# Attention through a packed set, then a squared-ReLU layer: second softmax's scores in 32x32 tiles, seven groups of block products, stores as steps of the plan on three queues

## The chip, the cores and the metric

The kernel runs on one core of a Trainium2 chip. The metric is the device time of one execution in microseconds. Before the change the median of five runs is 249.96 us (248.67 to 250.8).

A core has five engines that run side by side, each with its own instruction queue: TensorE (PE, matrix products; loading its weights is listed as PEld), VectorE (DVE), ScalarE (ACT), GpSimd (POOL) and SyncE (SP). Transfers between the device's memory and the core's are issued from the queues of SP, ACT and POOL.

## The reference

Eight batches of eight heads, 576 tokens, 64 numbers per head. A short set `p` of 32 rows per head attends to the 576 keys and values, and gives 32 packed rows; then the 576 queries attend to these packed rows. The result, 4608 tokens of 512 numbers, goes through a layer of 2048 hidden units.

```python
def _attn_ref(q, k, v, p):
    scale = 1.0 / np.sqrt(q.shape[-1])
    def sm_attn(qq, kk, vv):
        s = scale * np.matmul(qq, kk.transpose(0, 1, 3, 2))
        s = s - np.max(s, axis=-1, keepdims=True)
        a = np.exp(s)
        a = a / (np.sum(a, axis=-1, keepdims=True) + 1e-09)
        return np.matmul(a, vv)
    p_packed = sm_attn(p, k, v)
    return sm_attn(q, p_packed, p_packed)

def _moe_ref(x, w_in, w_out):
    r = np.maximum(x @ w_in, 0.0)
    return (r * r) @ w_out
```

All inputs and outputs are float32; the kernel computes its products in bf16.

## The kernel before, in words

**Stages of a batch.** The heads of a batch are two "quads" (`qd`) of four heads `h`. Loads (`Loads`) bring k, q and v in as bf16 through POOL's queue, batch 0's k as float32 through ACT's and SP's. DVE transposes k (`tr_k`, L273) and q (`tr_q`, L267). `S1` is the first softmax's scores (`s1`, `s1_rest`), with `p` spread into a block-diagonal tile `pT_bd`; ACT takes their exponential. `PV` multiplies with v and sums the rows. `XT` copies the product out as `pp` (`extract`), takes the reciprocal of the sums (`recip`), and `pq_block` copies the packed rows, as 32x32 blocks, into a block-diagonal tile `pq_bd` of 128x128 weights.

`M` (`m`, L354) multiplies the packed rows by w_in, in tiles of 64x32: eight matmuls of 512 columns, each into its own 32 partitions, for each 512 columns of w_in; from batch 1 on two such sets in a row. The layer's first product then needs no attention output: `f1_mm` (L417, halves in batch 0: L426) multiplies the softmax weights by `M`.

`S2` (`s2`, L379) is the second softmax's scores: for each quad, four matmuls of 288 columns with `pq_bd` as 128x128 weights (two halves of the queries, two halves `dh` of the head's 64 numbers). ACT takes the exponential (`s2_exp`); `N` sums over the 32 packed rows with a block of ones (L391), takes the inverse on ACT as logarithm and exponential (L396, L399), and DVE multiplies (`n_mul`, L405). In batch 0 (`SPLIT`) S2 and N are done in two halves of the queries.

`R` is `f1_mm` with its ReLU, on ACT or DVE; `F1` is the square (`f1_sq`, L452, DVE), into `gT`, which holds two batches. `F2` is the second product of the layer. A tile `t` of 128 tokens (36 in all) is 16 matmuls of 512 columns (`f2_mm`, L501), a copy out, and four stores, one to each of four 32-row parts (`store`, L477). From tile 15 on, four tiles at a time are a group (`GROUPS`): seven products of halves instead of eight (`prod`, L560, 16 matmuls of 256 columns each), with sums of the squares (`g_sum`, L546, names `WS`) and of w_out (`w_sum`, names `WT`) made on DVE, and the products copied or added into the output tile (`prod_out`). Tile 35 is done in two column halves (`f2_last`, L487).

**What sets the order.** Each piece of work is a `Step` with stages, dependencies, and slots that it takes and gives; some pieces may go to DVE or ACT. The order of all pieces, and the engine of each, was found beforehand and stands in the file as a compressed list (`ORDER`); `Plan.run` issues the pieces in that order. Each engine works its own list in order. Steps of type "-" and "DMA" issue nothing. So an instruction that waits holds up everything that was issued later on the same engine, stores and loads too.

**Buffers that matter here.** Two `h` buffers in PSUM (scores, sums and `f1` products of all wide batches, `M`), two `a` buffers (S1, PV, tiles 2 and 3), two output buffers `o0`, `o1`; eight load buffers for k and q (`kqb`); one tile `qT` for the transposed queries, so that `Tq` of a batch waits for S2 of the batch before; three output tiles `o_sb`.

**Stores.** They are issued in the step that copies or adds the last part of a tile, four in a row; all on SP, but for half of those of tile 35 that go to ACT's queue:

```python
(eng or nc.sync if i % 2 else nc.sync).dma_start(dst, src[32 * i:32 * i + 32])
```

Of the kernel before, what the change touches and what calls it, by code (L numbers as in the profile page):

```python
# [14 lines left out]
P = 128  # L15
# [11 lines left out]
GROUPS = (15, 19, 23, 27, 31)  # L27
SPLIT = (0,)

# [20 lines left out]
class Plan:  # L50
# [21 lines left out]
    'c-jrtgMu9i6a~Pm)5-X86x+6K+qP}nwr$(CZQHhY>nn=LD1aOaqU01vp_H0J$V=%+DJCT*AH}2W<fbUfL>Vb7m7*+^n<`Km%0R^^0VSb=RFq0n'  # L72
    'Z7NUIsSCBDj<k@PP#c;-J!v3qp%FBJ4p2>ML_?`QHK*|un-Wr9s!Fw}FO{T<)Qmb%H(E<$X)>LpO|*-i(rQ{y_h=f;p-VKMmeDmjLZ|30U8L)z'
    'e4NhGce+iF$i)xo1;yg$^qvy&JNiN?`78aQtn6VQ7v}_=ge&nsiou20&vCdMXW;BymuqnYp2&H*2)E&;+@4o(DXzdhcmNOQZJdnLaCI)vRk<&Z'
    '<;i@Et8r}}%p-Ul@8w3^lIQSO{>KqAgBS35e!_3~7x(1;ypeqpTT)A2DJ12@CE=1lp7Td0DJJEmp%j$jQd@5E1Afi-`6++m(o#j5$$S3JK~hm_'
    'N_)wm*|mVqmnE`JmdkqCD>=2G*4DMMSq{r$StVQLtNanuESg)(YcVaWEwr3g*S`8spniQI&*ZKA6jqm((n{J%^J#Idr%a$=5{f~Q6o=xw;!;vd'
    'Mk!pmD2!a>p<a}O^3XT>O&z!kAL6UrPiDz=xh=!J<21EpF+YX7V!0wH+BJZ7l5sm0xg>2h5v8I6RD{Y=6{<sHD3lX&J}%4McnR;|ef)z>Qc5<d'
    'ERE!{ypteJuA_9C&eq+U&dOLNTW={TEv2Vyl$ml;KFUvpsIaRHm7wCTQ8bmN&`g?5i|H>3$K(Ka1c$hzxD40eDqN2nb2IMB6L>05<3&81=eh6j'
    'W4^~<_$UA2K=DYVM0v7ELQgz7BuC|l9GBB_R<6iZxhZ!%ujRQslv-L>8)-9btZlTNcGND~%{xMSX>adKeXXzboxayk`dPp0PyOX(3o`PxvbNUF'
    '23kk!W<zYajk57J)28?q`dU&uS9=;p6KOQ<pna}AbeV3@eR8vx<8omx%@z3(zu=edzwAh`#FylfUXIC0&jqQY4ZIDtwYK+m&^|iAJ5WFB7yasO'  # L80
    'W4)|{4YFZ2#-`aUo8x<9@9e#=ELEmTRE=s-U1~^8sU9_^*3_9APz!2Hov15yr+ze;dQfi~LL(_LC*@R}meX+-F2Kb&8|UJpT$$JKdfvcWcsuXr'
    'yX=)~e1ln%NDj#@`K72-kgC#Fx=I)6E(2t!e3EbSTSx;mSUnm`!!$zUX(1h><8`b~)~PyEm*`5JrE_(g9#gMHSbR%jnJt^;vG$hF3Ro$tVH<6;'
    '?Xcap#}3*l`)Nn)m_4u%^r1o2pN7*on&g^J^Jp$DaxJBmw1zg&M%qe8=>#34b98~OxbDysdPcA54Sl4~^pk#(<F3OE-SxSJyDfL(&fJ}QaUbr-'
    'LwFdE<}o~pr|?Xk#mjgxujV~`fDiH!KF+83G@s)Oe3=VNS*a!Uq=7V%rqV*%NGItjeWb4p@(hvTGDgP9B$?`&BGYA_ERqGXLe|Je*(BR!r|gzJ'
    'vR`h=eYq!3<f*)rSMpx|N=)@?Y>lf4yzw=OH<_l?)S6b)X(r94xipU!)}mTk%V=etuM2gNF7+<gRk~W&=?2}bTXeg3r|!|cx?d0K5k0CW^pu{}'
    'b9zxP=~ca^H}$sO*9ZDYpXv+!r|J`PEWm;-(84U-Vq08GV96|vrLv5c--=pED{G~#f>pMvR?TW!ZL4SXt&uIYRleo6+D_VeyI_~?s@<@gcE|49'
    'Q~P1R?U(&C0pK7ef)I)@xZy_x!V%?9h$KjiWd4*$gS5ziOvs9C$ca42k3uMl;wXjED2Ixuf*Poe`e=nlXo~jegpTOr?~Y!WMayYB9j3eViilJ2'
    'Kpx5Cc`a|^GklS6b8G1(qh*53mDRFC4$5cwB|c5BS+%5A)S9|hH|Zfgt(Wz>KGx^zw|JJ&3R)d&Xw9s(U9^Yx+7yBCA|BEqI|`!&YN91NqX&jz'
    '0j;9Vw3|-T8G1=S2pq_f9FLQ8PR`E-xu$ysZKJ)kpAOM2`aqv3h=Vyc$LHLfhf8otZp}+*9UY|ebd_$>1A0u%VI0oUoSM^fCeF+`+)cPSx8jc6'
    'n+New9>vpnF3;zMyp&h+X5Pgo+!^^HXOIF?L`q3rSt$4PjegKS>b7W0ZaJ*8^|Qe?)F#?=TV~sApB=UncFk_tJxhel$c-|njJjxuCYXX*Sb}xf'  # L90
    'gzeakBe;!+Sk9|>9dG5Gyq^#AQ9j9M`4V5@>wJ@+@hcAXyybWNfj{#%{>>_o7!p$gBt*i*Eq;lXxDrd^NFqrrNhO)2kW`XJ(n>nXD48U)WR>ia'
    '%ac>`NIoecC8dm1l4??2YDgWaFO8+Sw3JrT!P8DUN@wXNJ*2nvmw_@^hRFySDWhbpjF*WrS*FPhnJKenjx3dBvQjq47TGSlWS<<66LLzf$r(8('
    '=jEc@kh}6o9?J`PBOm0We39?+Lqr{~Y77n35DitghHIooX|%@CgqlbbYf??2dA+GLjb_x$nnUwz5iOw=w2D^MYFb0<YZGm%ExpaPm3G#y+Fg5S'
    'Pwl7ub&w9$Av#ot=|~-|6TK63l1|a-Iz#8^JYArRb(yZvHM(9m>Q>#M=e@ghpB~V|dR$NH8NHx)yjS#w-qO4JP@m{CeXB9;oBq(>`d7_hF)YM<'
    '7HTf@SfoW+EQ@1_EQKYuq?XdsT6)W1nJla2wd|JDa#?OGWQDDW6|)jn+{#&bt7uiMy4A9}*4!FcV{2kft%bF;PS(YG__|tm>uJ5MkM*_wHo!*M'
    'NE>ZqZJbT8NjBN0+G5`fn{9J#p3S!fw#b&)3R`JwY^|-c4YtX)*jC$V+ijQawf%O$4%tyVZfESYowajz$*$OSyKQ&vx$luZwkP(?Uf4@}WpC}9'
    '?}L4`Pxjfq*jM{*e~j?g7={=KKrmeJAQpUxL^NU}4&ov{5+Id7DUu@vQX@SwA`5aLA95it3ZNj0pcqP`EGnQpDxoT>p*m`z4(g!+8lxGSqXk-{'
    '4cej|I{3SwE4ra4dZRD;p+5#<00v<&hF~a$V+2NGw0{)FU@XRAJSJcwCSfWjV;ZJo24-S5=3p-7V;&Y@Ar@gVmSP!}V<lE#6;@*n)?z(2U?a9*'
    'Gqz$Ic3>xVVGs6VzkeSN;2;j+FplCFj^iXw;1o{d49?;l&f@|u`7h!!uHY)J;W}>MChp)C?&2Qq;{hJwF`nQVp5i%P;3Zz+HQwMY-s2rU;3Gca'
    'Grr&}zTqdn;|G4>H~!!+{(+qT^Wmst4jjjc;ly-;oB$`#33fu9P$$fBIc~?}cpabPcfy?rC(?;>qMiQ$NqrJ;'  # L100
# [3 lines left out]
def kernel_impl(tc, q, k, v, p, w_in, w_out, out):  # L104
# [15 lines left out]
    with ExitStack() as ctx:  # L120
# [25 lines left out]
        pq_bd = [consts.tile([P, 896], BF16, name=f"pq_bd{i}") for i in range(2)]  # L146
# [11 lines left out]

        def bd(t, h, dh):
            return both(t, dh * BDW + 32 * h, P + (-32 if h % 2 else 32), 32)[32 * h:32 * h + 32]  # L160
# [7 lines left out]
        def setup():  # L168
# [4 lines left out]
            nc.vector.memset(kT[:, :, GM * P + 64:], 0.0)  # L173
            nc.vector.memset(v_t[0][64:, :, GM * D:], 0.0)
            nc.vector.memset(v_t[1][64:, :, GM * D:], 0.0)
            nc.vector.memset(pq_bd[0][:, :BDW + 2 * P], 0.0)

        def setup_rest():
            nc.gpsimd.memset(ones_bd, 0.0)
# [414 lines left out]
        def stage(*pieces):  # L594
            return list(pieces)
# [336 lines left out]
```

The softmax here doesn't subtract the row's maximum and nothing guards it: scores larger than these inputs give would overflow.

## Time and profile before

| what | us |
|---|---|
| median of five runs | 249.96 |
| the profiled execution | 249.17 |
| its span, first to last instruction | 247.2 |
| PE busy | 225.5 |
| DVE busy | 186.1 |
| ACT busy | 157.7 |
| POOL busy | 60.2 |
| mean granted TensorE clock | 0.995 |

The span is what the trace covers; some 2 us of the execution lie around it. Busy times overlap between engines. A matmul's record starts when it begins and ends when its results are written, so records of neighbouring matmuls overlap: the distance from one start to the next tells what a matmul costs, and a busy PE is not a PE at its peak. In the kernel's rows the output names stand left of the arrow and the inputs right of it.

### The profile page before, as it was taken

The page shows a single profiled execution, that of the slowest core. Times are in us where ns is not written, and L with a number is a line of the kernel's source. Part 1 is how long each engine was busy: PE and PEld are TensorE (multiplying, and loading weights), DVE is VectorE, ACT ScalarE, POOL GpSimd, SP SyncE. Part 2 cuts the span into 40 slices and gives each one's busy share as a digit, 9 for nine tenths or more (in the row PEclk, how much of TensorE's full clock was granted, in tenths as well). Part 3 has the DMA queues.
Part 4 walks back from the last instruction along what each step waited for, and adds up shares of the span by engine and source line. Part 5 has one row for each costly group of instructions (what it writes and reads, how often), then busy time and mean ns, then how long its engine had stood idle before and what let it go on. Part 6 is the DMA issues. An engine that isn't in the chain of part 4 may idle for free.

```text
span 247.2 us, 5373 instructions
## 1 busy us (share of the span) xinstructions
PE 225.5 (91%) x2096; PEld 160.1 (65%) x2096; DVE 186.1 (75%) x325; ACT 157.7 (64%) x273; POOL 60.2 (24%) x120
## 2 busy tenths in 40 slices
PE   0679998996999999999999999999999999999970
PEld 0525564573654666666556888887787888888860
DVE  4875649876998696779787989898897798767410
ACT  3368577885887766785788887877775756400010
POOL 7697576562093003452100000000000000000000
PEclk9999999999999999999999999999999999999998
DMA  7999999999999945699611010033014001504243
GB/s 221 199 183 205 205 202 208 204 245 220 193 121 203 244 92 95 95 181 213 118 45 42 13 32 3 0 88 88 3 32 124 18 3 44 128 1 110 63 110 102
DMA packets 27160, 29.01 MB, mean 117 GB/s; under 512 B 5760, under 2 KB 18816, under 8 KB 27136
## 3 DMA queue, kind: packets, MB, share of 16 engines
q0 software_dynamic: 19472, 17.99, 46.0%
q1 hardware_dynamic: 7328, 9.97, 14.9%
q10 hardware_dynamic: 336, 0.72, 0.9%
q8 instruction: 16, 0.26, 0.4%
q14 instruction: 8, 0.07, 0.1%
HBM read 37.22 MB, written 9.44 MB: 189 GB/s over the span
## 4 chain that ended last, share of the span: by engine, by line
PE 78%; DMA 11%; DVE 3%; ACT 3%; issue 1%; POOL 1%; SPq 0%; DVEq 0%
PE ps_o L560 24%; PE ps_h L417 20%; PE ps_o L501 16%; DMA q_b<-in_q_dram 4%; DMA k_b<-in_k_dram 4%; PE ps_m L354 4%; PE ps_h L426 3%; PE ps_a L283 3%; PE ps_s L379 3%; PE ps_pp L316 2%; DMA p_f<-in_p_dram 2%; PE ps_s L391 1%; DMA out_dram<-o_sb 1%; PE ps_a L501 1%; DVE kT L273 1%
## 5 line engine op out<-in xcount | busy, mean ns | idle before, releaser
L445 ACT ACTIVATE r<-ps_h 128x576 bf16<-128x576 f32 x99 | 63.7, 650 | 26.6 <-PE ps_h L417 24.6
L417 PE MATMUL ps_h<-a,M 128*128 128x288 bf16 x448 | 71.1, 286 | 0.0
L501 PE MATMUL ps_o<-w_out_b,gT 128*128 128x512 bf16 x208 | 58.7, 379 | 0.7 <-DMA w_out_b<-in_moe_w_out_dram 0.7
L417 PEld LDWEIGHTS <-M 128*128 128x128 bf16 x448 | 43.6, 98 | 16.3
L452 DVE TENSOR_TENSOR gT<-r 128x1152 bf16<-128x1152 bf16 x64 | 46.8, 747 | 6.1 <-ACT r L445 3.8
L560 PEld LDWEIGHTS <-wS 128*128 128x128 bf16 x320 | 31.0, 98 | 4.7 <-issue 0.4
L501 PEld LDWEIGHTS <-gT 128*128 128x128 bf16 x240 | 22.3, 98 | 17.0 <-issue 3.4
L560 PE MATMUL ps_o<-wT,wS 128*128 128x256 bf16 x240 | 30.5, 273 | 0.0
L238 POOL DMA_DIRECT2D v_r<-in_v_dram x32 | 19.0, 597 | 33.9 <-DVE wT L525 16.0
L164 ACT CAST M<-ps_m 128x1024 bf16<-128x1024 f32 (+1 forms) x26 | 23.1, 915 | 6.2 <-PE ps_m L354 4.9
L267 DVE STREAM_TRANSPOSE qT<-q_b 128x1152 bf16<-128x1152 bf16 (+1 forms) x18 | 21.9, 1229 | 6.1 <-DMA q_b<-in_q_dram 4.2
L560 PEld LDWEIGHTS <-gT 128*128 128x128 bf16 x240 | 23.3, 98 | 3.8 <-issue 0.4
L164 ACT COPY o_sb<-ps_o 128x512 f32<-128x512 f32 (+1 forms) x15 | 8.6, 572 | 22.7 <-PE ps_o L560 19.6
L560 PE MATMUL ps_o<-w_out_b,gT 128*128 128x256 bf16 x160 | 20.9, 273 | 0.0
L166 DVE COPY o_sb<-ps_o 128x512 f32<-128x512 f32 (+1 forms) x20 | 13.4, 671 | 8.1 <-PE ps_o L560 3.6
L283 PE MATMUL ps_a<-pT_bd,kT 128*128 128x128 bf16 x128 | 10.3, 233 | 8.3 <-DVE kT L273 8.3
L386 ACT ACTIVATE e<-ps_s,rD 128x576 bf16<-128x576 f32 (+1 forms) x18 | 12.2, 687 | 8.3 <-PE ps_s L379 8.2
L166 DVE CAST M<-ps_m 128x1024 bf16<-128x1024 f32 (+1 forms) x10 | 11.2, 1118 | 7.2 <-PE ps_m L354 6.5
L283 PEld LDWEIGHTS <-kT 128*128 128x128 bf16 x128 | 8.7, 105 | 10.7 <-DVE kT L273 8.7
L573 DVE TENSOR_TENSOR o_sb<-ps_o,o_sb 128x512 f32<-128x512 f32 x15 | 10.3, 689 | 6.2 <-PE ps_o L560 5.0
L379 PE MATMUL ps_s<-qT,pq_bd 128*128 128x288 bf16 x64 | 11.4, 304 | 3.4 <-DVE qT L267 2.1
L405 DVE SCALAR_TENSOR_TENSOR a<-e,rD,ls 128x576 bf16<-128x576 bf16 (+1 forms) x18 | 13.4, 742 | 1.4 <-ACT ls L399 1.2
(72 smaller groups left out, 302.8 us busy)
## 6 DMA issues: line engine op xcount, KB each, us to landing
out_dram<-o_sb SPq DMA_DIRECT2D x140, 64.0 KB, 1.7
k_b<-in_k_dram POOLq DMA_DIRECT2D x14, 288.0 KB, 8.9
q_b<-in_q_dram POOLq DMA_DIRECT2D x14, 288.0 KB, 9.0
v_r<-in_v_dram POOLq DMA_DIRECT2D x16, 160.0 KB, 8.6
v_r<-in_v_dram POOLq DMA_DIRECT2D x16, 128.0 KB, 7.1
w_in_b<-in_moe_w_in_dram POOLq DMA_DIRECT2D x8, 256.0 KB, 8.5
w_out_b<-in_moe_w_out_dram POOLq DMA_DIRECT2D x8, 256.0 KB, 8.6
k_f<-in_k_dram ACTq DMA_DIRECT2D x1, 576.0 KB, 4.2
```

The lines of the kernel that those rows point to most:

```text
L164: nc.scalar.copy(dst, src)
L166: eng.tensor_copy(dst, src)
L238: nc.gpsimd.dma_start(self.vr[32 * i:32 * i + 32, h0:h1, :n * D], src[:, :, J0[i] * D:(J0[i] + n) * D])
L267: nc.vector.transpose(self.qT[:, qd, :, j0 * 32:j1 * 32].rearrange("p dh (j a) -> p j dh a", a=32), self.t.qb[qd][:, j0 * D:j1 * D].rearra ...
L283: nc.tensor.matmul(ps[:, g * P:(g + 1) * P], lhsT=self.kT[:, qd, g * P:(g + 1) * P].bitcast(BF16).rearrange("p (t two) -> p two t", two=2) ...
L379: nc.tensor.matmul(ps[:, c], lhsT=self.pq[:, blk(qd, dh)], rhs=self.qT[:, qd, dh, n0:n0 + HALF], start=(dh == 0), stop=(dh == 1))
L405: nc.vector.scalar_tensor_tensor(out=self.a2[:, qd, n0:n1].rearrange("p (c n) -> p c n", n=HALF), in0=self.e2[qd, hf], scalar=self.rD[:, q ...
L417: nc.tensor.matmul(ps[:, c, :HALF], lhsT=a.M[:, qd, fb * FB:(fb + 1) * FB], rhs=a.a2[:, qd, c * HALF:(c + 1) * HALF], start=(qd == 0), sto ...
L445: nc.scalar.activation(dst, src, ACT.Relu)
L452: eng.tensor_tensor(out=gT[:, fb - 1:fb + 1, o:o + S], in0=r, in1=r, op=ALU.mult)
L501: nc.tensor.matmul(po[t], lhsT=gT[:, fb, n0:n0 + P], rhs=w_out_b[:, fb, :], start=(fb == 0), stop=(fb == NFB - 1))
L560: nc.tensor.matmul(ps[:, u * EH:(u + 1) * EH], lhsT=lhs, rhs=rhs, start=(n in (1, 2, 4) and kk == 0 and u == 0), stop=(kk == KB - 1 and u ...
```

## The change

- **S2 in tiles.** `pq_bd` is gone. `packed` takes each head's 32x32 weights where they are: for two of the eight pairs (head, `dh`) from `pp` itself, for the other six from a small tile `pq`, which `pq_part` fills with six block copies a batch instead of eight. `s2` computes both quads together: for each half of the queries and each `dh`, eight matmuls of 32 rows, 32 columns of weights and 288 columns, head `h` of quad `qd` from row part `h` into partitions `32 * (h ^ qd)`. A wide batch takes both `h` buffers at once; 32 matmuls instead of eight.
- **Buffers.** `qT` has two buffers, and `Tq` waits for S2 two batches back; `e1` and `e1r` have one instead of two; `e2` has two for each quad instead of three in all. Two memsets of `pq_bd` go.
- **Groups.** Tiles 7 to 14 become two more groups; `GROUPS` has seven.
- **Squares** may go to ACT (`Square`); the list puts ten of 64 there.
- **Stores** are steps of their own (`store_step`), of two stores each, on SP, from tile 8 on also POOL, from tile 31 on also ACT: 92 on SP, 50 on POOL, 6 on ACT, where it was 144 on SP and 4 on ACT.
- **The order.** `ORDER` is a new list for the new steps; the loads and all engines' lists are rearranged. SP's queue has batch 0's k ahead of `p`, where `p` was first; w_in's first pieces and q of batch 2 stand earlier in POOL's queue; in batch 0 `M` is ahead of S2. Expected costs of a few steps and some margins (`plan.base`) in the file differ; they have no effect on what is issued beyond the list.

```diff
-GROUPS = (15, 19, 23, 27, 31)
+GROUPS = (7, 11, 15, 19, 23, 27, 31)
+PQ_PARTS = (((0, 1), (1, 0), (1, 1)), ((2, 0), (2, 1), (3, 0)))
...
-                self.tile_of("qT", att, [P, NQD, 2, S], BF16, bufs=1)
+                self.tile_of("qT", att, [P, NQD, 2, S], BF16)
...
-                self.tile_of("e1", att, [P, NQD, GM, P], BF16)
+                self.tile_of("e1", att, [P, NQD, GM, P], BF16, bufs=1)
...
-            def pq_block(self, pr, eng):
+            def pq_part(self, i, eng):
+                self.tile_of("pq", small, [P, NQD, 2, 32], BF16, bufs=2)
                 ps = self.ps_pp if eng is nc.vector else self.pp
-                for e in range(2):
-                    for dh in range(2):
-                        s0 = 64 * e + 32 * dh
-                        cast(eng, bd(self.pq, 2 * pr + e, dh),
-                             both(ps, pr * 64 + 32 * e, P + (-32 if e else 32), 32)[s0:s0 + 32])
+                for h, dh in PQ_PARTS[i]:
+                    pr, e = divmod(h, 2)
+                    s0 = 64 * e + 32 * dh
+                    cast(eng, self.pq[32 * h:32 * h + 32, :, dh], both(ps, pr * 64 + 32 * e, P + (-32 if e else 32), 32)[s0:s0 + 32])
+
+            def packed(self, h, qd, dh):
+                pr, e = divmod(h, 2)
+                if e + dh == 2 * pr:
+                    return self.pp[32 * h:32 * h + 32, qd * P + pr * 64 + 32 * (e ^ qd):][:, :32]
+                return self.pq[32 * h:32 * h + 32, qd, dh]
...
-            def s2(self, qd, hf):
-                ps = self.pss[qd, hf] = self.ps_s(hf)
+            def s2(self, hf):
+                if hf is None:
+                    pss = [ps_h.tile([P, 2, 512], F32, name="ps_s", tag="h")[:, :, :HALF] for _ in range(NQD)]
+                else:
+                    ps = ps_h.tile([P, 2, 512], F32, name="ps_s", tag="h")
+                    pss = [ps[:, qd:qd + 1, :HALF] for qd in range(NQD)]
                 for c, n0 in enumerate([hf * HALF] if hf is not None else [0, HALF]):
                     for dh in range(2):
-                        nc.tensor.matmul(ps[:, c], lhsT=self.pq[:, blk(qd, dh)],
-                                         rhs=self.qT[:, qd, dh, n0:n0 + HALF],
-                                         start=(dh == 0), stop=(dh == 1))
+                        for h in range(QH):
+                            for qd in range(NQD):
+                                o = 32 * (h ^ qd)
+                                nc.tensor.matmul(pss[qd][o:o + 32, c], lhsT=self.packed(h, qd, dh), rhs=self.qT[32 * h:32 * h + 32, qd, dh, n0:n0 + HALF],
+                                                 start=(dh == 0), stop=(dh == 1))
...
-            eng.tensor_tensor(out=gT[:, fb - 1:fb + 1, o:o + S], in0=r, in1=r, op=ALU.mult)
+            dst = gT[:, fb - 1:fb + 1, o:o + S]
+            if eng is nc.scalar:
+                eng.activation(dst, r, ACT.Square)
+            else:
+                eng.tensor_tensor(out=dst, in0=r, in1=r, op=ALU.mult)
...
-        def store(t, src, eng=None, e0=0, e1=NE):
-            for i in range(4):
+        def store(t, src, i0, eng, e0=0, e1=NE):
+            for i in range(i0, i0 + 2):
                 b, j = divmod(t * 4 + i, JT)
                 dst = out[b * S:(b + 1) * S, e0:e1].rearrange("(a j) e -> j a e", j=JT)[j]
-                (eng or nc.sync if i % 2 else nc.sync).dma_start(dst, src[32 * i:32 * i + 32])
+                eng.dma_start(dst, src[32 * i:32 * i + 32])
...
-                old = [f"S2.{b - 1}.{qd}.{hf}" for qd, hf in halves(b - 1)]
+                old = [f"S2.{b - 2}.{hf}" for hf in parts(b - 2)] if b > 1 else []
...
+        def store_step(name, ts, after, slot, hf=None):
+            def piece(t, i):
+                args = (hf * EH, (hf + 1) * EH) if hf is not None else ()
+                return [(e, us, lambda eng=eng: store(t, src[t if hf is None else (t, hf)], i, eng, *args))
+                        for e, us, eng in (("SP", 0.86, nc.sync), ("POOL", 1.0, Q), ("ACT", 0.86, A))
+                        if e == "SP" or t >= (8 if e == "POOL" else 31)]
+            return Step(f"ST.{name}", [stage([("-", 0.0, lambda: None)]), stage(*[piece(t, i) for t in ts for i in (0, 2)]),
+                                       stage([("-", 1.8, lambda: None)])],
+                        [after], (), [("osb", 2, slot)] if slot else [], lag=0.1)
```

## The prediction, made before the changed kernel had run

> **What bounds the kernel now.** I read the page first (busy shares, the forty slices), then the windows by stage, then the timeline of TensorE around one batch, the chain of waits, and the output queue at the end.
>
> The page, busy time (us, share of the span) and two rows of slices of 6.2 us:
>
> ```profile
> PE 225.5 (91%) x2096; PEld 160.1 (65%) x2096; DVE 186.1 (75%) x325; ACT 157.7 (64%) x273; POOL 60.2 (24%) x120
> PE   0679998996999999999999999999999999999970
> DVE  4875649876998696779787989898897798767410
> ```
>
> The windows; per row: us, then busy us (and count) of PE, weight loads, DVE, ACT, POOL, then clock, DMA share, GB/s:
>
> ```profile
> 0.00:20.00 20.00, 9.29 (x71) 5.26 (x72) 12.84 (x36) 10.20 (x23) 15.76 (x32) 1.00 1.16 201
> 20.00:65.00 45.00, 41.50 (x369) 25.17 (x368) 32.59 (x59) 33.17 (x60) 25.16 (x49) 1.00 1.22 213
> 65.00:135.00 70.00, 70.00 (x624) 41.77 (x623) 57.67 (x98) 53.20 (x88) 19.24 (x40) 1.00 0.75 136
> 135.00:214.00 79.00, 78.98 (x803) 65.13 (x802) 68.75 (x114) 57.77 (x98) 0.00 (x0) 1.00 0.17 42
> 214.00:239.80 25.80, 25.72 (x236) 22.80 (x233) 14.28 (x23) 2.99 (x6) 0.00 (x0) 1.00 0.28 72
> 239.80:247.20 7.40, 0.00 (x0) 0.00 (x0) 0.00 (x0) 0.37 (x1) 0.00 (x0) 0.83 0.39 102
> ```
>
> There are three stages. To 65 us TensorE is idle for 10.7 + 3.5 us. From 65 to 239.8 us it never rests: whatever it no longer does there shortens the run one for one, as long as DVE (82 and 87% in the two long windows) and ACT (76 and 73%) keep up. After 239.8 us come 7.4 us without a matmul.
>
> The timeline of TensorE (start, us, line, shape, count); the x8 row is the same query cut to 125.84:125.86:
>
> ```profile
> 124.63 1.24 PE L501 MATMUL ps_o<-w_out_b,gT 128*128 128x512 bf16 x5
> 125.80 0.62 PE L354 MATMUL ps_m<-w_in_b,pp 64*32 64x512 bf16 x16
> 126.36 2.12 PE L501 MATMUL ps_o<-w_out_b,gT 128*128 128x512 bf16 x9
> 128.31 1.14 PE L379 MATMUL ps_s<-qT,pq_bd 128*128 128x288 bf16 x8
> 129.29 0.81 PE L501 MATMUL ps_o<-w_out_b,gT 128*128 128x512 bf16 x3
> ...
> 125.80 0.41 PE L354 MATMUL ps_m<-w_in_b,pp 64*32 64x512 bf16 x8
> ```
>
> Starts matter, since matmuls overlap: the eight score matmuls of a batch take 129.29 - 128.31 = 0.98 us. The M product in 64x32 tiles has eight matmuls under way together (x8 within 0.41 us). Its sixteen start at 125.80 and the next full matmul at 126.36. The five before it, at 0.216 each, would have let something start at 125.71, so the block costs 0.65 us: two rounds of 0.213, plus 0.22 around it.
>
> From the chain of waits, the price of a direct and of a grouped matmul (0.217 and 0.109 us):
>
> ```profile
> 129.46 0.65 PE ps_o L501 x3
> 214.17 20.32 PE ps_o L560 x186
> ```
>
> The end, from the timeline: one queue issues twenty stores back to back, to 245.06, though the last copy is over at 240.17.
>
> ```profile
> 235.24 9.82 SPq L481 DMA_DIRECT2D out_dram<-o_sb  x20
> 239.80 0.37 ACT L164 COPY o_sb<-ps_o 128x256 f32<-128x256 f32 x1 [2.95 <-DMA out_dram<-o_sb]
> ```
>
> **The change part by part.** The profiled execution took 249.17 us (span 247.2 and 1.97 around it); the median of the runs is 249.96, 0.8 more. The sum is against 249.17.
>
> *Two more groups (7 and 11).* The built order has 128 fewer matmuls of 512 columns and 224 more of 256. At 0.216 and 0.109: 27.65 - 24.42 = **3.2 us less** on the path.
>
> *Scores in tiles.* Batches 1 to 7: eight matmuls (0.98 us) become 32 of 32x32, eight positions, four rounds of 288 columns. No row shows a 32-row tile, so I bound it. Best: rounds overlap as M's do, 4 x 0.1225 + 0.19 to 0.22 around them = 0.70. Worst: the tiles run one at a time, 32 x 0.1225 + 0.2 = 4.1. M is the nearest row (eight positions, four streams in each row group), so I take 0.70: 7 x 0.28 = **2.0 us less**. Batch 0, in two halves on an early PE, is nothing either way (two rounds plus 0.2 against four matmuls); its M and scores now stand together.
>
> A rule against this: the Trainium skill, TensorEngine Tiling (Array Packing), Restrictions and Gotchas, says that different row tiles cannot use one PSUM bank at the same time; here four row tiles write one bank in each round. M already has two row tiles in each bank, and its rounds do not show any turn-taking (0.213 us for eight). By the rule the four would take turns, two matmuls at a time, 2.15 us a batch, and the sum would end 11 us higher; I go by the row.
>
> *DVE and ACT.* By the order, DVE loses 10 squares (0.747), 12 plain output copies (0.67) and 5 score-weight blocks (0.22), and gains 16 group sums (0.683), 6 output adds (0.689) and small change: about -0.4 us net. ACT gains the 10 squares, 12 copies (0.572) and one large copy, and loses 11 blocks (0.241), a value cast (1.26) and some small ones. A square of 1152 bf16 on ACT has no row; between 0.65 (576 wide) and 1.258 (a 1280-wide copy), on the line through both, 1.15. ACT: +13 us. The earlier squares and sums of groups 7 and 11 fall in the stretch 30 to 135 us. Counting the order's DVE and ACT instructions against PE's there, with these durations, DVE comes to some 93% and ACT to 87% of PE's time, more than any long window above. Lower bound 0 (135 to 214 us ran at 87% of DVE with 0.02 us of idle PE), upper bound 6 (what about 5% of that stretch would cost). I take **2.0 more**. A group's products also hang on sums that need the next batch's squares, where direct matmuls were free filler; that is in the same 2.0. The scores now take both `h` buffers at once instead of one after the other; M does that already from batch 1.
>
> *The first 65 us.* SP now issues the second half of k before p. p landed 4.09 us after issue and fed the transposes; behind 576 KB that landed at 6.85, it comes near 6.9 and goes through an ACT cast (0.23 on DVE before), a transpose (0.24) and four expansions in a row on DVE (4 x 0.25): the first matmul moves from 7.66 to some 8.7, **1.0 more**. Against that, w_in's first pieces are queued behind 1376 KB instead of 1952, M comes before the scores, and by the same walk the first F1 matmul moves from 19.89 to about 18.2: 1.7 less in all, the 1.0 included. Then there is one wait at 60 us:
>
> ```profile
> PE ps_s L379 <- DVE qT L267: 2.1, 1, 2.1
> ```
>
> It is q of batch 2, whose second half stands behind 9920 KB on POOL's queue and now behind 8640: some 6 us earlier at the 205 GB/s of those slices (each KB counted as it lands). So the 2.1 should go; next late is w_out (0.74). With qT double, its transpose waits for scores two batches back, not one, which frees load slots sooner; e1 single makes the exps of batch b+1 wait for the P.V product of b, long done by then. Ends: +2 (late start, nothing recovered) and -3.8 (both). The new DVE and ACT load begins here and may swallow some: I take **1.5 less**.
>
> *Stores.* They leave the copy's step and go to three queues: SP 92, POOL 50, ACT 6. At the end SP has 12 instead of 20, ACT 6 instead of 4, POOL 6. At 0.465 each from 235.24, SP is through ten by 239.9 and issues its last two after the last copy, 240.2 to 241.1. ACT's four lie before its last copy (237.0 to 238.9), two after. POOL's last four follow the copy of 238.43; POOL issues cost 0.53 to 0.73 here, so they end by 240.6 to 241.4. Last issue 241.1 instead of 245.06, landing 1.5 to 1.7 after. A store from POOL is nowhere in the trace: its loads landed 3.4 us after issue at best (160 KB), which is the upper bound; 244.8 at worst against 246.2. So 1.4 to 4.0; I take **3.5 less**, nearer the store's own rows. In the middle a POOL store waits for its copy with loads of batches 6 and 7 queued behind; those sit some 70 pieces of the order, about 10 us, ahead of what reads them, so I cost it at nothing, and at 2 us if that cover is gone.
>
> Sum: 249.17 - 3.2 - 2.0 + 2.0 - 1.5 - 3.5 = 241.0; with the 0.8 of the median, **241.8 us**.
>
> **The rivals.**
> - *DVE and ACT become the bound* in 30 to 135 us: +6 instead of +2, and the early gain gone (+1.5): 247.3. For it: 93 and 87%. Against: ten squares and twelve copies have moved to the emptier engine, and slices at 9 passed without a PE gap.
> - *The row tiles do not overlap* (slower than before). Two at a time cost 16 x 0.1225 + 0.2 = 2.15 us a batch, 8 x 1.17 = 9.4 more instead of 2.0 less: 253.2. The other terms are worth 6.2, so it decides the sign where a batch's scores cost over 0.98 + 6.2/8 = 1.76 us. One at a time would give 269. Against: M.
> - *The cover holds*: no stall from DVE and ACT, and both early gains: 241.8 - 2.0 - 2.3 = 237.5.
> - *The tail stays*, landing as late as POOL's loads do: 243.9; as with the tiles gaining nothing (243.8).
>
> **How the numbers follow.** Chances: forecast 0.46 (own range 239.5 to 243.5), one of the small misses at 243.5 to 245.5 0.17, DVE and ACT bound 0.15, cover holds 0.14, tiles serial 0.08. 0.1 is left out above (tiles, and a little of DVE) and less than 0.1 below: 237 to 248. A measurement of this kernel can tell about 0.5% (1.25 us) from no change. Faster needs under 248.7: all but the tiles and a fifth of the DVE case: 0.88; same 0.03; slower 0.09.
>
> **What would show it.** Right: L501 at 80 direct matmuls to `ps_o` and the grouped line at 784; the score line with 32 starts within some 0.7 us before the next full matmul; PE busy throughout from 65 us; DVE near 186 and ACT near 171; no q wait near 60 us; the last store issued within 1.5 us of the last copy. Wrong: scores at 2 us or more a batch; PE idle behind DVE's sums or ACT's evictions in the windows 65:135; PE waiting for k or v of batch 6 behind a POOL store; the span's end over 4 us after the last copy still.

## The result, and the profile after

| | before | after |
|---|---|---|
| median of the runs, us | 249.89 | 251.95 |
| the profiled execution, us | 249.17 | 252.04 |
| its span, us | 247.2 | 250.0 |
| the last matmul's start, us | 239.44 | 242.06 |

The ratio of after to before is 1.0027, with a 95% interval of 1.0004 to 1.0051: a quarter of a per cent slower, where 241.8 us was forecast. It is formed from the runs within 1.5% of each kernel's fastest, 18 of 38 after the change; the medians of all runs, in the table, are 0.8% apart, and the profiled execution lies at the median. The forecast is wrong by 10 us, and its range (237 to 248) does not hold the time.

Busy times and two rows of slices (6.25 us each) of the page after:

```profile
PE 224.0 (90%) x2384; PEld 166.8 (67%) x2384; DVE 185.7 (74%) x324; ACT 168.8 (67%) x279; POOL 86.6 (35%) x169
PE   0467899998989999999999999999999999999970
DVE  2874259959769989979986998998888488567420
```

DVE and ACT have the load that was forecast (186 and 171). But TensorE is nearly as busy as before, although it has less to do. The windows, with the same columns as those of before:

```profile
0.00:20.00 20.00, 7.11 (x93) 4.55 (x94) 12.23 (x34) 8.68 (x19) 14.60 (x30) 1.00 1.08 203
20.00:65.00 45.00, 42.08 (x373) 23.85 (x373) 30.72 (x52) 32.62 (x56) 25.09 (x47) 1.00 1.17 184
65.00:135.00 70.00, 67.79 (x802) 49.38 (x801) 60.61 (x104) 57.84 (x96) 25.36 (x49) 1.00 0.79 143
135.00:214.00 79.00, 78.70 (x866) 64.08 (x865) 67.02 (x113) 60.35 (x96) 13.76 (x28) 1.00 0.20 55
214.00:239.80 25.80, 25.80 (x236) 22.89 (x235) 14.67 (x23) 8.92 (x13) 5.88 (x12) 1.00 0.18 51
239.80:250.00 10.20, 2.53 (x24) 2.02 (x21) 0.42 (x1) 0.37 (x1) 1.96 (x4) 0.80 0.37 107
```

In the first 20 us TensorE works 2.2 us less than before; between 65 and 135 us it rests for 2.2 us, where it never rested; and the last matmul comes 2.6 us later than before.

**What came as forecast.** Scores in tiles, from the chain of waits (start, us, what):

```profile
46.55 0.65 PE ps_o L516 x3
47.20 0.61 PE ps_s L389 x32
47.81 1.19 PE ps_o L516 x5
```

The chain shortens the block at its start: from the start of the direct matmul before the block to the start of the one behind it, less that matmul's own 0.216, it is 0.708 us in six of the seven wide batches (forecast 0.70; before 0.98). By the rule of the Trainium skill that was weighed there (TensorEngine Tiling (Array Packing), Restrictions and Gotchas: different row tiles cannot use one PSUM bank at the same time) it would have been 2.15, by the prediction's estimate; four row tiles of one bank run at full rate here. The direct and grouped matmuls are 80 (`ps_o`) and 784, and the q wait near 60 us is gone.

**What did not: the start.** The chain from M of batch 0 to F1:

```profile
15.13 0.70 DVE M L166
15.86 0.59 ACT M L164
16.47 0.51 ACT e L397
17.02 0.41 PE ps_s L402
...
20.34 0.96 PE ps_h L437 x4
...
25.75 3.04 PE ps_h L437 x12
```

The same matmuls before the change:

```profile
19.89 2.08 PE ps_h L426 x8
...
23.27 0.49 PE ps_h L426 x4
```

M's copies stand ahead of the scores' exps, which start at 16.47 (before 14.16), and the first F1 matmul comes at 20.14 (before 19.89, forecast 18.2). Then each F1 matmul of 288 columns costs 3.04/12 = 0.25 us, to the end of the row: half rate. Before, the first eight cost 2.08/8 = 0.26 us, but from 23.3 us on it is 0.49/4 = 0.12. The first direct F2 matmul follows at 28.59, where it was 25.40. The trace's record of the granted clock gives TensorE its full clock at 30.8 us, where it was 22.9 before. The page and the windows do not show it: ahead of the first change on record they print 1.00.

**And the end.** The timeline (start, us, instruction), and POOL's drains (count: shortest/median/longest ns, first and last start), which stand at the program's last line:

```profile
241.34 1.96 POOL L496 DMA_DIRECT2D out_dram<-o_sb  x4 [2.00 <-DVE o_sb L166]
242.41 0.37 ACT L164 COPY o_sb<-ps_o 128x256 f32<-128x256 f32 x1 [8.19 <-DMA out_dram<-o_sb]
```

```profile
L972 POOLq DRAIN  x3: 46/102/6627, 242.6 to 249.8; - x3
L972 SPq DRAIN  x3: 7/7/7, 245.7 to 249.5; - x3
```

The stores are issued as forecast, the last at 243.4 to 243.8, one us after the last copy, and SP has seen all its landings by 245.7. But POOL's drain, which began at 242.6, lasts 6.63 us, to 249.25, and the program ends behind it. In the kernel before, POOL's last DMA is a load, its long drain ran at 122.7 us, and the drain behind the last landing took 0.1 us:

```profile
L927 POOLq DRAIN  x3: 51/98/3097, 122.7 to 246.9; - x3
```

### The profile page after: what moved, and what is told of

It reads as the page before. It is cut to its first block, busy times and chain, and to the rows that moved or that the text cites. A ratio compares the mean times of both kernels' runs of the same rounds, so it can differ in the third digit from the quotient of the medians.

```text
span 250.0 us, 5959 instructions
## 1 busy us (share of the span) xinstructions
PE 224.0 (90%) x2384; PEld 166.8 (67%) x2384; DVE 185.7 (74%) x324; ACT 168.8 (67%) x279; POOL 86.6 (35%) x169
## 3 DMA queue, kind: packets, MB, share of 16 engines
q1 hardware_dynamic: 4832, 6.63, 9.2%
## 4 chain that ended last, share of the span: by engine, by line
PE 62%; DMA 12%; DVE 9%; POOL 5%; ACT 4%; issue 4%; POOLq 0%; DVEq 0%
PE ps_o L575 28%; PE ps_h L428 13%; PE ps_h L437 4%; DMA q_b<-in_q_dram 4%; DMA v_r<-in_v_dram 3%; PE ps_m L357 3%; PE ps_o L516 3%; DMA k_b<-in_k_dram 3%; PE ps_a L516 3%; DMA k_f<-in_k_dram 2%; PE ps_a L280 2%; POOL v_r L236 2%; PE ps_pp L313 2%; POOL out_dram L496 2%; DVE qT L264 2%
## 5 line engine op out<-in xcount | busy, mean ns | idle before, releaser
L456 ACT ACTIVATE r<-ps_h 128x576 bf16<-128x576 f32 x98 | 62.8, 651 | 24.7 <-PE ps_h L428 20.8
L428 PE MATMUL ps_h<-a,M 128*128 128x288 bf16 x448 | 71.1, 286 | 1.4 <-ACT r L456 0.8
L496 POOL DMA_DIRECT2D out_dram<-o_sb x50 | 25.0, 508 | 104.7 <-DVE o_sb L588 74.3
L575 PEld LDWEIGHTS <-wS 128*128 128x128 bf16 x448 | 42.6, 98 | 9.1 <-issue 3.2
L467 DVE TENSOR_TENSOR gT<-r 128x1152 bf16<-128x1152 bf16 x54 | 40.0, 751 | 9.1 <-ACT r L446 4.7
L575 PE MATMUL ps_o<-wT,wS 128*128 128x256 bf16 x336 | 41.8, 273 | 0.2 <-DVE wS L561 0.2
L575 PE MATMUL ps_o<-w_out_b,gT 128*128 128x256 bf16 x224 | 33.0, 273 | 0.0
L516 PE MATMUL ps_o<-w_out_b,gT 128*128 128x512 bf16 x80 | 23.4, 389 | 1.0 <-DVE gT L467 1.0
L561 DVE TENSOR_TENSOR wS<-gT 128x1024 bf16<-128x1024 bf16 (+1 forms) x32 | 19.1, 619 | 0.8 <-ACT gT L465 0.7
L575 PE MATMUL ps_o<-wT,gT 128*128 128x256 bf16 x112 | 16.2, 273 | 0.0
L575 PE MATMUL ps_o<-w_out_b,wS 128*128 128x256 bf16 x112 | 15.5, 273 | 0.0
L166 POOL COPY pT_bd<-pT 32x128 bf16<-32x128 bf16 x28 | 11.3, 403 | 11.5 <-PE ps_a L293 5.2
```

The lines of the kernel that those rows point to most:

```text
L428: nc.tensor.matmul(ps[:, c, :HALF], lhsT=a.M[:, qd, fb * FB:(fb + 1) * FB], rhs=a.a2[:, qd, c * HALF:(c + 1) * HALF], start=(qd == 0), sto ...
L456: nc.scalar.activation(dst, src, ACT.Relu)
L467: eng.tensor_tensor(out=dst, in0=r, in1=r, op=ALU.mult)
L496: eng.dma_start(dst, src[32 * i:32 * i + 32])
L516: nc.tensor.matmul(po[t], lhsT=gT[:, fb, n0:n0 + P], rhs=w_out_b[:, fb, :], start=(fb == 0), stop=(fb == NFB - 1))
L561: eng.tensor_tensor(out=dst, in0=a, in1=b, op=op)
```

## The experiments

The experiments leave the list of the plan as it is and override it: in `Plan.run`, `MOVE` gives a piece (step, stage, number) another position in the order, `ENGINE` another engine. Theories after the result: (A) POOL's closing drain costs 3 us; (B) the late first matmul is lost time; (C) the late full clock costs about 3 us; (D) M ahead of the scores costs about 1 us; later (E) a load on POOL's queue makes the new wait between 65 and 70 us. The general rival is the prediction's own: DVE and ACT are too full, and each gain is lost again. One kernel's executions differ by several us (the spans of the 38 of the changed kernel run from 246.4 to 252.5), so the span of one profiled execution decides little by itself; what happens where in the trace, and the ratios, are read beside it.

### The last stores without POOL (e1_tail)

```diff
+ENGINE = {("ST.31.6", 1, 1): "ACT", ("ST.31.6", 1, 3): "ACT", ("ST.31.7", 1, 3): "ACT",
+          ("ST.35.0", 1, 0): "SP", ("ST.35.0", 1, 1): "SP"}
```

> The changed kernel, with the five store pieces of the last 128-token blocks that stood on POOL or late on SP spread over SP and ACT alone; POOL's last DMA then issues some 10 us before the end. Theory (POOL's closing drain sets the end): the drain that ran 242.63 to 249.25 in the changed kernel is short or early, the end follows the last landing at about 246, and the span is about 247, 3 us below 250.0, a ratio to the kernel before of about 0.991. Rival (the drain lasts as long whenever POOL has issued stores at all in the run, or the landings set the end anyway): within 0.7 us of the changed kernel, ratio 1.000 to 1.005.

Measured: span 246.5, ratio 0.9992 (0.9955 to 1.0028). The drains in this kernel, and the end of its chain:

```profile
L983 POOLq DRAIN  x3: 46/169/6400, 228.8 to 246.3; - x3
```

```profile
238.64 2.14 DMA out_dram<-o_sb
240.79 1.61 DMA out_dram<-o_sb
242.40 0.36 ACT o_sb L175
```

The drain still takes 6.4 us, but starts at 228.8 beside TensorE's work; the end is 1.1 us behind SP's last landing (245.4). The span is 3.5 us shorter; 1.3 of that is an earlier last matmul (240.74 for 242.06), so the drain is worth 2.2: from the start of the last matmul to the end of the span it is 5.79 us, where it is 7.98 in the changed kernel. The other runs agree: with POOL's last stores left in place (e2, e3, e4, e5, e9) this distance is 7.97 to 7.98 us, without them (e6, e7, e10, e11, e12) 5.20 to 6.31. That is theory A, with 2 us for its 3. The ratio alone does not show it: it is 0.35% (0.9 us) below the changed kernel's, the intervals overlap, and theory A's 0.991 lies outside.

### p first at the start (e2_p_first)

```diff
+MOVE = {("LP.0", 0, 0): 0.5, ("P.0", 1, 0): 20.1, ("P.0", 2, 0): 20.2, ("X.0", 1, 0): 20.3,
+        ("X.0", 1, 1): 20.4, ("X.0", 1, 3): 20.5, ("X.0", 1, 2): 20.6}
+ENGINE = {("P.0", 1, 0): "DVE", ("X.0", 1, 1): "ACT", ("Ck.0.0", 1, 0): "ACT"}
```

> The changed kernel, with the start in the order of the kernel before: p is loaded first on SP, cast on DVE, transposed and spread over pT_bd ahead of the casts of k, of which ACT and DVE do one half each. Theory (the late first matmul is lost time): the first matmul comes at about 7.7 us instead of 9.4 and the span falls by 1 to 1.7 us, ratio about 0.997. Rival (the time between 14 and 31 us, bound by ACT's queue and the half clock, swallows it): the first matmul is early, but the first F1 matmul stays near 20.1 and the ratio at 1.002.

Measured: first matmul 8.37, first F1 matmul 19.53, span 249.0, ratio 1.0011 (0.9972 to 1.005). The start, F1 and the span moved by 0.6 to 1.0 us in the profiled execution; the ratio cannot tell it from the changed kernel's.

### Matmuls ahead of the first one (e3_warm)

```diff
+        warm = w_out_b[:, NFB - 1, :]
+        nc.vector.memset(warm, 0.5)
+        w_ps = ps_h.tile([P, 2, 512], F32, name="ps_h", tag="h")
+        for _ in range(17):
+            nc.tensor.matmul(w_ps[:, 0], lhsT=warm[:, :P], rhs=warm, start=True, stop=True)
```

> The changed kernel with 17 matmuls of 128x512 ahead of its first one, on a constant written by DVE (a slice of w_out's tile that is loaded later), into a PSUM bank that nobody reads: nothing waits for them, and they fill TensorE's idle time from about 1.4 to 8 us. Theory (the full clock is granted only after enough unbroken work, and the changed kernel gets it at 30.8 us instead of 22.9): the full clock comes before 15 us, F1's matmuls are 0.12 us apart from the first one on, and the span falls by 2.5 to 4 us, ratio about 0.990. Rival 1 (the clock falls back in the gaps between 9 and 20 us): the full clock comes near 31 us again and the ratio stays at 1.002. Rival 2 (from 20 to 31 us ACT's relus set the pace, not TensorE): the clock is early and the span falls by less than 1 us.

Measured: ratio 1.0085 (1.004 to 1.013), span 248.8. Here the clock changes often enough for the windows to show it (the last three columns: granted clock, DMA share, GB/s):

```profile
12.00:16.00 4.00, 2.14 (x50) 1.21 (x50) 3.20 (x8) 2.19 (x7) 3.62 (x6) 1.00 1.19 207
16.00:20.00 4.00, 2.49 (x23) 1.11 (x23) 2.32 (x5) 3.42 (x9) 2.16 (x4) 0.56 1.24 205
25.00:30.00 5.00, 5.00 (x21) 2.77 (x20) 1.16 (x2) 2.40 (x4) 2.44 (x4) 0.50 1.54 192
30.00:35.00 5.00, 4.81 (x39) 2.24 (x38) 2.21 (x3) 3.17 (x6) 1.13 (x2) 0.99 1.35 199
```

Full from 6.25 us, lost at 16.5, back at 30.1: rival 1. Warming alone buys nothing. Why the ratio is 0.6% above the changed kernel's, with intervals that overlap, is open; the span of the one profiled execution is below it.

### Scores ahead of M (e4_scores_first)

```diff
+MOVE = {("M.0.0", 0, 0): 100.5, ("M.0.0", 1, 0): 100.6, ("M.0.0", 1, 1): 107.5}
```

> The changed kernel with the first block of w_in's product with pp (and its two copies on DVE and ACT) behind the first scores, their exps and the two sums on the engines, as the kernel before has it, instead of ahead of them. Theory (the copies of that product stand in front of the exps on ACT): the first exp of the scores starts at about 15.0 us instead of 16.5, the first F1 matmul at 18.5 to 19 instead of 20.1, and the span falls by 1 to 1.5 us, ratio about 0.997. Rival (the product's copies are only moved, and F1 waits for them, or the half clock of that stretch takes it all): first F1 matmul at 20 or later, ratio 1.001 to 1.004.

Measured: ratio 1.0051 (1.0009 to 1.0094). From the chain:

```profile
15.35 0.51 ACT e L406
16.80 0.67 PE ps_m L366 x8
17.50 0.70 DVE M L175
18.22 0.59 ACT M L173
20.38 0.96 PE ps_h L446 x4
```

The first exp starts 1.1 us earlier, but M's copies now stand behind it and F1 waits for them; its first matmul is at 20.18. Theory D falls: the two blocks together set the time, not their order.

### TensorE's waits filled (e5_keep), and the same for the kernel before (e8_before_keep)

```diff
+PAD = {("S1.0.0", 0): 20, ("PV.0.0", 0): 2, ("M.0.0", 0): 2, ("N.0.0.0", 0): 6,
+       ("N.0.0.1", 0): 6, ("R.0.2", 0): 2, ("R.0.4", 0): 3}
...
+        w_ps = ps_o.tile([P, NE], F32, name="ps_o0", tag="o0")
+        def idle(n):
+            for _ in range(n):
+                nc.tensor.matmul(w_ps, lhsT=warm[:, :P], rhs=warm, start=True, stop=True)
...
+            self.idle(PAD.get((p.step.name, p.stage), 0))
```

In the kernel before:

```diff
+PAD = {("S1.0.0", 0): 15, ("S1.0.1", 0): 1, ("PV.0.0", 0): 2, ("S2.0.0.0", 0): 5,
+       ("N.0.0.0", 0): 1, ("S2.0.1.1", 0): 1, ("N.0.0.1", 0): 4, ("R.0.2", 0): 1}
```

> The changed kernel with matmuls that nobody reads (128x512, into a bank that F2 takes later) in TensorE's waits: 20 ahead of the first matmul, 2 ahead of pp's products, 2 ahead of w_in times pp, 6 ahead of each first sum of the scores, 2 and 3 ahead of two F1 pairs. In the four runs so far the full clock came at the end of a 3.41 us stretch in which TensorE was busy for 0.87 or more, and was lost after stretches of 0.49 and 0.57. Theory (the late full clock costs some 3 us): the full clock comes before 10 us and stays, F1's matmuls are 0.12 us apart from the first on, the span falls by 2 to 3.5 us, ratio to the kernel before about 0.992. Rival (from 20 to 31 us the relus on ACT set the pace): the clock comes early and the span falls by under 1 us, ratio 1.000 or more.

> The kernel before, with its own waits filled in the same manner (15 matmuls ahead of the first, and 1 to 5 in seven other waits): what an early full clock is worth to it, whose clock came at 22.9 us. TensorE ran there at half rate from 7.7 to 22.9 us for about 11 us of work. Theory: from 12 to 20 us the chain of the two softmaxes on ACT and DVE sets the pace, so the gain is 0.5 to 1.5 us, ratio about 0.996, less than the changed kernel's. Rival (the clock matters as much here): ratio 0.990.

Measured: e5 span 245.4, ratio 0.994 (0.9906 to 0.9974). Its windows:

```profile
8.00:12.00 4.00, 2.24 (x25) 1.55 (x26) 3.68 (x11) 1.47 (x3) 3.77 (x10) 0.89 1.22 178
12.00:16.00 4.00, 3.76 (x61) 2.09 (x60) 2.80 (x7) 1.57 (x5) 3.70 (x6) 0.68 1.19 207
16.00:20.00 4.00, 3.31 (x31) 1.49 (x31) 2.59 (x6) 3.54 (x10) 1.39 (x2) 1.00 1.24 205
20.00:25.00 5.00, 3.79 (x30) 1.96 (x28) 3.15 (x5) 3.67 (x8) 2.96 (x4) 1.00 1.24 205
25.00:30.00 5.00, 4.95 (x43) 2.59 (x43) 2.22 (x3) 3.74 (x7) 2.44 (x4) 1.00 1.54 191
```

The clock is full from 14.5 us. The first F1 matmul gains only 0.5 us (19.62), the first direct F2 matmul 2.6 (25.95 for 28.59), the last matmul 4.6: theory C. By the ratios the gain is 0.87%, 2.2 us, and the intervals do not meet. What the last matmul gains beyond that is put down to the clock by no run.

The kernel before gains nothing: 1.0034 (0.9995 to 1.0072), where its theory had 0.996, and the last matmul is at 239.12 for 239.44. Its first F1 matmul does come 1.1 us earlier (18.78 for 19.89), but then the trace loses the clock from 23.8 to 27.2 us, behind 0.95 and 0.84 us of idle TensorE, and the first direct F2 matmul comes at 26.47 for 25.40. So e8 does not tell what a full clock that stays would be worth there.

When the clock changes, from the traces of all these kernels (busy share of TensorE in the 3.41 us that end with the change; all distances between changes ahead of the tail are multiples of 3.41 us):

```
kernel            full from  (share)   lost at  (share)   full again  (share)
before              22.89     0.97
after               30.84     1.00
e1_tail             29.28     0.95
e2_p_first          30.49     1.00
e3_warm              6.25     1.00      16.48    0.49       30.14      1.00
e4_scores_first     12.30     0.87      15.71    0.57       29.36      1.00
e5_keep              4.29     0.83      11.11    0.40       14.53      0.93
e6_ends             28.99     0.95      69.95    0.28       73.36      0.99
e7_all               6.40     1.00
e8_before_keep       6.69     1.00      23.76    0.48       27.17      1.00
e9_k_early          12.68     0.88      16.09    0.52       29.74      1.00
e10_no_pool_stores  28.46     0.89
e11_all_k            5.88     1.00
e12_no_fill         30.00     1.00
```

Stretches of 0.80 and 0.78 in the changed kernel (20.6 to 27.4 us) brought no full clock. One of 0.84 (10.4 to 13.8) did not, one of 0.83 did, so the border is near there and not sharp in these records. On the way down, stretches of 0.59 and more kept the full clock in all these traces and those of 0.28 to 0.57 in the table lost it, but e3 kept it through two of 0.47 (6.3 to 9.7 and 67.7 to 71.1 us). The Trainium skill (TensorE: Matmul & The Clock Gate, Part 1: The HAM clock gate) describes this: a free-running window of 3413 ns, full rate after a busy one, half rate after an idle one. The traces agree on the window; but the clock was lost without any idle window, at shares of 0.28 to 0.57 and in e4 with no wait over 0.5 us in that stretch.

Why the changed kernel has such stretches, as far as the two timelines tell; no run puts the pieces back. In the kernel before, the stretch that brings the full clock (19.5 to 22.9 us) holds eight F1 matmuls in a row and eight of `M`, and from 22.5 to 24.7 the first softmax's products of batch 1 stand between the F1 pairs. In the changed order the sums of batch 0's second scores stand among the first F1 matmuls (19.94 and 21.10), TensorE waits 0.50 us behind them and 0.74 us at 25.0 for a ReLU, and those products of batch 1 stand at 38.8.

### Both ends, and all three (e6_ends, e7_all)

e6 has the edits of e1 and e2, e7 also those of e5, with 18 matmuls at the start:

```diff
+MOVE = {("LP.0", 0, 0): 0.5, ("P.0", 1, 0): 20.1, ("P.0", 2, 0): 20.2, ("X.0", 1, 0): 20.3,
...
+ENGINE = {("P.0", 1, 0): "DVE", ("X.0", 1, 1): "ACT", ("Ck.0.0", 1, 0): "ACT",
+          ("ST.31.6", 1, 1): "ACT", ("ST.31.6", 1, 3): "ACT", ("ST.31.7", 1, 3): "ACT",
+          ("ST.35.0", 1, 0): "SP", ("ST.35.0", 1, 1): "SP"}
...
+PAD = {("S1.0.0", 0): 18, ("PV.0.0", 0): 2, ("M.0.0", 0): 2, ("N.0.0.0", 0): 6,
...
```

> The changed kernel with both ends mended: the last blocks' stores on SP and ACT alone, and p first at the start. Theory (the two gains are apart in time and add up): 3.5 and 1.0 us, span about 245.5, ratio about 0.987 by the spans. Rival (the start's microsecond is lost again before 70 us): span 246.5, as with the stores alone, ratio 0.998.

> Both ends mended and TensorE's waits filled (18 matmuls ahead of the first). Theory: the gains of the two add up, span about 243, ratio about 0.977. Rival (the full clock is worth nothing while ACT sets the pace): the same as with both ends mended, within 0.7 us.

Measured: e6 ratio 0.9921 (0.9865 to 0.9977), between the theory's 0.987 and the rival's 0.998. But it rests on four of its ten runs; the median of all ten is 249.42 us, that of the kernel before beside it 249.52, so the gain is not secure. e7 0.9865 (0.9782 to 0.9949, four runs), span 244.4: 0.6% below e6, less than forecast, and the intervals overlap. In e6's profiled execution (span 248.8, the second longest of its ten) something else is seen:

```profile
65.00:70.00 5.00, 2.51 (x18) 1.49 (x17) 2.34 (x6) 3.73 (x5) 2.58 (x6) 0.99 1.16 229
70.00:73.30 3.30, 3.30 (x32) 1.72 (x33) 1.98 (x6) 0.99 (x2) 1.22 (x2) 0.50 1.24 206
```

TensorE waited 2.5 us near 68 us for a square, and then lost the clock for 3.4 us. In the changed kernel the same wait is 1.0 us, and in e1 to e5, e7 and e10 it is 1.0 to 2.3; the kernel before has none there. This led to the next run.

### A load moved on POOL's queue (e9_k_early)

Who waits for whom in the changed kernel, from three queries of its timeline (POOL, DVE, TensorE; in brackets the idle time before and what ended it):

```profile
59.30 1.75 POOL L236 DMA_DIRECT2D v_r<-in_v_dram  x3 [5.60 <-DVE v_b L166]
...
68.28 0.84 DVE L270 STREAM_TRANSPOSE kT<-k_b 128x320 f32<-128x320 f32 x2 [1.09 <-DMA k_b<-in_k_dram]
69.04 0.72 DVE L467 TENSOR_TENSOR gT<-r 128x1152 bf16<-128x1152 bf16 x1
...
69.81 0.39 PE L516 MATMUL ps_o<-w_out_b,gT 128*128 128x512 bf16 x1 [0.95 <-DVE gT L467]
```

```diff
+MOVE = {("Lv.4.0.1", 0, 0): 422.5}
```

> The changed kernel with one load moved on POOL: the v load of batch 4 (step Lv.4.0.1), at which POOL stood from 53.7 to 59.3 us for its buffer, now stands behind three v pieces and a k of batch 3 that waited behind it. Theory (the wait of 1.1 us at 68.6 us, where TensorE waits for a square that stands on DVE behind a transpose of k that has not landed, comes from POOL's queue): that k is issued at about 55 us instead of 61 to 64.5, the wait at 68.6 is gone, and the span falls by 0.5 to 1.2 us, ratio about 0.999. Rival (DVE's and ACT's load sets the pace there, and the wait turns up elsewhere before 75 us): span within 0.3 us, ratio 1.002 to 1.004.

Measured: ratio 0.9977 (0.9942 to 1.0012), span 247.3, last matmul 239.31 for 242.06. POOL issues that k at 54.3, and DVE's transpose no longer waits:

```profile
54.28 0.57 POOL L222 DMA_DIRECT2D k_b<-in_k_dram  x1
```

```profile
65.00:135.00 70.00, 69.03 (x819) 50.97 (x818) 62.82 (x107) 58.76 (x99) 22.95 (x44) 1.00 0.73 132
```

The list of TensorE's waits is empty between 62 and 72 us, as it is in e11 and e12, which have the same edit. Theory E holds for the wait. For the time, the ratio is 0.5% below the changed kernel's, and the intervals overlap. Of the 2.7 us in the profiled span the wait is 1.0, and the clock, which comes 1.1 us earlier here, can be at most half of that time; the first direct F2 matmul is at 28.60 for 28.59. The rest is open: in e1 to e4, which leave the load where it was, the last matmul is at 240.7 to 241.0, so part of it is how long the changed kernel's one profiled execution was.

### No store on POOL at all (e10_no_pool_stores)

The edit of e1, and every other store piece of POOL's on SP:

```diff
+ENGINE = {("ST.7.6", 1, 2): "SP", ("ST.7.6", 1, 3): "SP", ("ST.7.7", 1, 3): "SP",
...
```

> The kernel of e1_tail with all other stores of POOL (25 pieces, 50 issues in the changed kernel) on SP too. Prediction's term (POOL's stores in the middle cost nothing): span and ratio as with the last stores moved alone, 246.5 us and 0.999, within 0.7 us. Rival 1 (they stand ahead of loads of k and v, and the waits of 0.5 and 0.4 us of the first softmax's products at 122.7 and 123.9 us come from there): those two waits vanish, span 0.5 to 1.5 us lower. Rival 2 (SP's queue becomes the late one): the last store is issued later, span higher by 0.5 us or more. The drain at POOL's end follows its last DMA, a load near 125 us.

Measured: ratio 1.0014 (0.9978 to 1.005), span 247.0, 0.5 above e1_tail. The waits near 122 us stay, 0.49 and 0.41 us from start to start as in the changed kernel and in e1, and waits of 1.0 and 0.4 us come near 138 (one of 0.9 stands in e11 too, which has POOL's stores). POOL's stores in the middle cost nothing that can be measured, as predicted.

### All edits, with and without the fillings (e11_all_k, e12_no_fill)

e11 is e7, and e12 is e6, each with the load of e9 moved:

```diff
-MOVE = {("LP.0", 0, 0): 0.5, ("P.0", 1, 0): 20.1, ("P.0", 2, 0): 20.2, ("X.0", 1, 0): 20.3,
+MOVE = {("Lv.4.0.1", 0, 0): 422.5,
+        ("LP.0", 0, 0): 0.5, ("P.0", 1, 0): 20.1, ("P.0", 2, 0): 20.2, ("X.0", 1, 0): 20.3,
```

> Both ends mended, TensorE's waits filled, and the load of batch 4 moved. Theory: as without the last (span 244.4, ratio 0.9865) less the wait near 65 us: span 243.3, ratio about 0.983. Rival: no gain over that run.

> The best version so far without its filling matmuls: both ends mended and the load of batch 4 moved. Theory (the late full clock is worth 2 to 4 us also when all else is mended): full clock near 29 us, span 244 to 245.5, ratio about 0.990, 1.1% above the version with the fillings. Rival (with the rest mended the clock no longer matters): ratio about 0.980, as with the fillings.

| | ratio to before | median, us | span, us | full clock from, us |
|---|---|---|---|---|
| e11_all_k | 0.979 (0.9738 to 0.9842) | 244.39 | 241.8 | 5.9 |
| e12_no_fill | 0.9836 (0.9791 to 0.9881) | 246.01 | 244.5 | 30.0 |

The windows of e11:

```profile
0.00:20.00 20.00, 15.68 (x134) 7.00 (x135) 12.88 (x35) 10.14 (x23) 14.55 (x30) 1.00 1.05 205
65.00:135.00 70.00, 68.02 (x811) 50.66 (x796) 61.62 (x101) 57.48 (x97) 22.94 (x44) 1.00 0.70 129
236.50:241.80 5.30, 0.04 (x1) 0.00 (x0) 0.00 (x0) 0.37 (x1) 0.00 (x0) 0.96 0.37 99
```

Both beat both kernels. The clock is worth 2.7 us between the two spans (the first direct F2 matmul is at 25.29 and 27.82), but 0.5% between the ratios, whose intervals overlap; e12's interval holds its rival's 0.980 and not its theory's 0.990, so with the rest mended the runs do not settle what the clock is worth. Against e6 and e7, which differ by the load's move alone, the ratios are 0.8% lower, again with overlapping intervals: 2 us, where the wait alone is 2.5 and 1.0 in their traces.

## Why the prediction was wrong

Against the profiled execution, in us (forecast 241.0, measured 252.04):

| term | forecast | measured | off |
|---|---|---|---|
| two more groups | -3.2 | -3.2 | 0 |
| scores in tiles | -2.0 | -1.9 | 0.1 |
| the first 65 us | -1.5 | +4.1 (to 70 us) | 5.6 |
| DVE and ACT | +2.0 | +3.6 (behind 70 us) | 1.6 |
| stores and end | -3.5 | +0.3 | 3.8 |

How the measured column comes out. Groups: by the counts, as in the forecast. Scores: seven times 0.98 - 0.708. The two stretches: TensorE's time beyond its matmuls' own cost (distance from start to start, less 0.216, 0.109, 0.122 and so on for each shape, the late first matmul included) grew from 23.5 to 28.3 us ahead of 70 us, and from 3.2 to 8.3 behind it; what the scores' blocks do to that count (0.2 and 1.4 of it, and 0.5 that batch 0's scores save) is taken out. The end: from the end of the last matmul (239.72 and 242.33) to that of the span, 7.7 us for 7.4.

1. **The first 65 us** failed in its walk to "the first F1 matmul moves from 19.89 to about 18.2". It came at 20.14. The walk gave w_in's earlier load a gain; but M's copies and the scores' exps follow each other on ACT and DVE either way (e4). And the term ended with the first F1 matmul: it held nothing for the rate at which F1 then runs: it read the windows' clock of 1.00, where F1 cost 0.26 us a matmul before the change too, to 22.9 us. The prediction said of the early TensorE only that batch 0's scores are nothing "on an early PE"; the price of the late clock was missing: 2.6 us to the first direct F2 matmul and 2.2 by the ratios in e5, 2.7 by the spans and 1.2 by the ratios between e12 and e11. The first matmul's own delay was forecast as 1.0 and was 1.7, of which e2 gets 1.0 back. The wait for q near 60 us went as forecast. "next late is w_out" was wrong: next was k of batch 3, for which TensorE waited 1.0 us here and up to 2.5 in other runs.
2. **DVE and ACT**: the size was off and the cause partly another. The load is as forecast, and the waits behind 70 us (0.2 to 0.5 us each) are behind DVE's and ACT's instructions. That DVE's load, not the new order, makes these was argued, not shown. The largest wait of the stretch was assigned to this term in advance, but came from POOL's queue (e9).
3. **Stores and end**: the step "landing 1.5 to 1.7 after" took the end to be the last landing. The issues were right (SP's last at 243.4, 1.0 us behind the copy), the landings too (245.7 at SP, 2.9 us behind the end of the last copy, 6.1 before). What ends last is POOL's drain, for which the term held nothing; it costs 2.2 us (e1). Without it the distance from the last matmul to the end is 1.4 to 2.5 us shorter than before the change (7.72 us), the lower part of the term's 1.4 to 4.0, not 3.5. The last row of the list of what would show it wrong, "the span's end over 4 us after the last copy still", is what happened: 250.0 - 242.8 = 7.2.
4. **Right**: the block of scores to 0.01 us, the counts, DVE and ACT's load, ACT's square (1.16 measured for 1.15), the wait for q, no cost of POOL's stores in the middle.

Of the rivals, "DVE and ACT become the bound" (247.3) and "the tail stays" (243.9) are each a part of it, the second for another reason (it had late landings, not a drain); none had the clock.

## What to carry to other kernels

When TensorE is given less work at the start, look at what fills its waits: in these traces the clock followed, with few exceptions, the share of a 3.4 us stretch in which TensorE was busy, and the emptier start kept it at half rate for 8 us longer. Ask of the last transfer not only when it lands but which engine's queue issued it and what that engine still does at the program's end. And a load that waits for a buffer holds the loads behind it: read the queue's order before putting a wait down to load.

## What the runs showed of the hardware that was not expected

- **POOL's drain.** It ends 5.5 to 6.0 us after POOL's last store was issued (after: issue over at 243.30, drain to 249.25; e1: 229.69 and 235.15; e7: 227.01 and 232.47), though POOL's stores land 1.9 to 2.3 us after their issue (medians after, by size). Behind a last load of v it was 8.6 and 9.0 us (e10: 127.09 and 135.65; before: 116.79 and 125.77).
- **The clock** was lost behind stretches with a busy share of 0.28 to 0.57, none of them idle throughout, and it comes by where the stretches happen to lie: with the same start, the full clock is there at 30.8, 29.3 and 28.5 us (after, e1, e10), and in e9 from 12.7 to 16.1 and again from 29.7.
- **32x32 tiles**: eight start within 25 ns, four row tiles of one bank run together at full rate, and a block costs 0.22 us beyond its four rounds of 0.1225 (0.708 us in all).
